# Attention fused with two dense layers: VectorE's splits, sums and weight conversion ordered behind evictions of scores, and dense work that starts one turn later

## The chip, the cores and the metric

One core of one Trainium2 chip. The metric is device microseconds of one execution. The kernel before has a median of 1105.09 us over 3 runs (1104.98 to 1105.69).

## What is computed

Inputs are q, k, v of 4 x 8 heads, 576 positions, 64 wide, and the weights of two dense layers. Everything is float32.

```python
scores = (1/8) * q @ k^T
scores = where(scores >= max(scores) - tau, scores, -1e9)
attn   = exp(scores - max(scores)); attn /= sum(attn) + 1e-9
x = (attn @ v), heads put side by side          # 2304 x 512
h = x @ w_in1;  x = where(h >= 1, h, where(h <= -1, 0, (h+1)^2/4)) @ w_out1
h = x @ w_in2;  x = (h * clip(h+3, 0, 6) / 6) @ w_out2
```

The dense layers go from 512 to 2048 and back to 512 features.

## The kernel before, in words

A dense product is made of three matmuls on operands that are each split in a high part (fp32r) and a low part. ScalarE makes the high part, VectorE or GpSimd subtracts it from the source for the low part.

**Attention** goes over 16 jobs (a batch and a pair of heads) of 5 steps each (four blocks of 128 queries, then the last 64 of both heads). One step: TensorE makes scores in two PSUM pairs P0 and P1 (`em_scores`, L380); VectorE evicts them to `p`, negated, with the row's maximum (L395: this is called an eviction below); ScalarE takes the exponential (`em_exp`, L408) and VectorE the threshold `th` (L411); VectorE masks and sums (`em_mask`, L417); TensorE transposes `p` (`em_pt`, `em_tail`, L294), ScalarE copies the result to `Gf` and `Gt` (L445, L448, L459, L463); every few steps ten pairs of matmuls multiply it by v (`pv_chunk`, L481). After a job VectorE adds 1e-9 to its sums `z` and inverts them (`pre_norm`, L500, L501). The scores of a step can't be written before the eviction of the step before has read the same PSUM pair.

**Dense work beside attention** (`dense1`, the first layer for the first three batches, in groups of 256 tokens): `split_x` splits x in `xh` (ScalarE, L704) and `xl` (VectorE, L705), four pairs in a round; `em_h` makes 12 matmuls of 256 columns into the one bank Q2 (L724), then ScalarE (L733, L734), VectorE (L735, tile `r`), ScalarE (`gh`, L741) and GpSimd (`gl`, L742) apply the gate; `em_part` multiplies by w_out (L786) into bank Q3, which is copied to `ob` when a round ends (L799 or L795). The next 12 matmuls of L724 can't begin before L735 has read Q2. Weights are converted on the way (`split_a`, `split_b`): ScalarE L124, L127, L145; GpSimd L128, L143, L147; VectorE L135 (shift) and L141 (sign).

**After attention** the rest of the dense work follows, with matmuls of 512 columns (L766, L1164 and others).

What sets the order: a scheduler in the framework places instructions by a model of time. `after(ins, prev)` adds an order without a semaphore ("ins not before prev" on the same engine). `pins` holds the last instruction of a kind: `S` the last exponential, `M` the last mask, `V` and `G` those of the dense gate. While attention runs, `split_x` put L704 behind `S` and L705 behind `M`; L135, L141 and L500 had no such pin on VectorE.

The main loop (`for _ in attention()`) gets a turn at every `yield` of attention. As soon as the four jobs of the first batch are done, `mode["mlp"]` is set and each turn gives `dense1` a credit of 0.57.

```python
for _ in attention():
    if not mode["mlp"]:
...
        if not ready(0):
            continue
        mode["mlp"] = True
    credit = min(credit + share, 3.0)
```

Of the kernel before, what the change touches and what calls it, by code (L numbers as in the profile page):

```python
# [11 lines left out]
ALU = mybir.AluOpType  # L12
# [6 lines left out]
def kernel(  # L19
# [89 lines left out]
            tc.add_manual_dep(ins.ins, prev.ins.name, mybir.DependencyInfo(kind, why), reason="pace")  # L109

    pe_pins = []
    pins = {"M": None, "S": None, "V": None, "G": None}

    def place_of(f, hl, dt, name):
        return (wbase if f < NF1 else wpool[f]).tile([128, 512], dt, tag=f"wi{hl}{f}", name=name)
# [1 line left out]
    def split_a(kind, m, f):  # L117
        t = wraw.pop((kind, m, f))
        pool = wbase if f < NF1 else wpool[f]
        hi = pool.tile([128, 512], F32R, tag=f"w{kind}h{f}", name=f"w{kind}h{f}")  # L120
        lo = pool.tile([128, 512], F32R, tag=f"w{kind}l{f}", name=f"w{kind}l{f}")
        c = stage.tile([128, 512], U32, tag="w_c", name="w_c", bufs=2)
        r = t[:, :, 0].bitcast(I32)
        x = S.activation(out=r, in_=t[:, :, 0], func=ACTF.Copy, scale=2.0 ** -29)  # L124
        after(x, pins["S"])
        if mode["att"]:
            after(S.activation(out=f32(c), in_=f32(t[:, :, 1]), func=ACTF.Abs), x)  # L127
            G.tensor_scalar(  # L128
                out=f32(c), in0=f32(c), scalar1=122879.9921875, scalar2=2.0 ** -15, op0=ALU.min, op1=ALU.max)
        else:  # L130
            S.activation(out=f32(c), in_=f32(t[:, :, 1]), func=ACTF.Abs)
            x = V.tensor_scalar(
                out=f32(c), in0=f32(c), scalar1=2.0 ** -15, scalar2=122879.9921875, op0=ALU.max, op1=ALU.min)
            after(x, pins["V"])
        V.tensor_scalar(out=c, in0=c, scalar1=3, scalar2=0x3FFFFFFF,  # L135
                        op0=ALU.logical_shift_left, op1=ALU.bitwise_and)
        wc[kind, m, f] = (hi, lo, c, t, r)

    def split_b(kind, m, f):
        hi, lo, c, t, r = wc.pop((kind, m, f))  # L140
        V.scalar_tensor_tensor(out=c, in0=t[:, :, 1], scalar=0xC0000000, in1=c,  # L141
                               op0=ALU.bitwise_and, op1=ALU.bitwise_or)
        x = G.tensor_tensor(out=c.bitcast(I32), in0=c.bitcast(I32), in1=r, op=ALU.add)  # L143
        after(x, pins["G"])
        x = S.activation(out=hi, in_=f32(c), func=ACTF.Copy)  # L145
        after(x, pins["S"])
        x = G.tensor_tensor(out=lo, in0=f32(c), in1=f32(hi), op=ALU.subtract)  # L147
        after(x, pins["G"])
        wsp[kind, m, f] = (hi, lo)
# [206 lines left out]
    def em_scores(j, i):  # L356

        last = i == NBLK - 1

        if not last:  # L360
            mode["s"] += 1
        ss = [unit_bank() for _ in range(1 if last else 2)]
        prev = None
        c = slice(i * 128, i * 128 + (TAIL if last else 128))
        thirds = j >= JR
        whole = thirds and last
        es = ((0, 0), (1, 1), (0, 1), (1, 0)) if last else ((0, 0), (1, 0), (0, 1), (1, 1))
        terms = ((qt, kt), (qt, kl), (ql, kt)) if thirds else ((qt, kt),)
        x = 0
        for pair in (((0, 0),), ((0, 1),)) if whole else (es[0:2], es[2:4]):  # L370
            for n, (a, w) in enumerate(terms):
                for h, e in pair:
                    r = slice(0, 128) if whole else slice(h * D, (h + 1) * D)
                    k0 = e * HS + (TAIL if last or h == 0 else 0)
                    if whole:
                        o, cs = ss[0][:, e, 0:HS], slice(MAIN, MAIN + 128)
                    else:
                        o, cs = ss[0][h * TAIL:(h + 1) * TAIL, e, 0:HS] if last else ss[h][:, e, 0:HS], c
                    with tc.high_priority(offset=900 if x else 0):
                        mm = T.matmul(o, a[j][r, cs], w[j][r, k0:k0 + HS], start=(n == 0), stop=(n == len(terms) - 1),  # L380
                                      skip_group_check=True)
                    after(mm, prev)
                    prev = mm
                    if x == 0:
                        pe_pins.append(mm)
                        for y in range(1 if last else 2):
                            after(mm, readers.get((mode["s"] - y) % 2), True)
                    x += 1
        nm = ap.tile([128, 2], F32, tag="nm", name="nm", bufs=3)
        th = ap.tile([128, 2], F32, tag="th", name="th", bufs=3)  # L390
        p = ap.tile([128, 2, 2, HS], F32, tag="p", name="p", bufs=3)
        if i == 0:
            zt[j] = ap.tile([128, 9], F32, tag="z", name="z", bufs=2)
        for x, s in enumerate(ss):
            reads(V.tensor_scalar(out=p[:, x], in0=s[:, :, 0:HS],  # L395
                                           scalar1=taus[:, 3:4] if j >= JR else -1.0, scalar2=3e38,
                                           op0=ALU.mult, op1=ALU.min, accum_out=nm[:, x:x + 1]), len(ss) - 1 - x)
        blk[j, i] = (p, nm, th, [])

    blk = {}  # L400
# [94 lines left out]
    def pre_norm(j):  # L495
        if j not in zt:
            return
        z = zt.pop(j)
        rz = rp[:, 0:9].unsqueeze(2) if j in OVER else ap.tile([128, 9, 1], F32, tag="rz", name="rz", bufs=2)
        V.tensor_scalar(out=z, in0=z, scalar1=1e-9, scalar2=None, op0=ALU.add)  # L500
        V.reciprocal(out=rz[:, :, 0], in_=z)  # L501
        rb = ap.tile([128, SEQ], F32, tag="rb", name="rb")
        if j in OVER:
            V.transpose(out=rq, in_=rp)
            rd = dram.tile([9, 128], F32, name=f"rd{j}")
            for a in range(4):
                nc.sync.dma_start(out=rd[:, 32 * a:32 * a + 32], in_=rq[32 * a:32 * a + 9, :])
            rbs[j] = (rd, rb)
            return
        rb = rb[:, 0:MAIN].rearrange("p (c h n) -> p c h n", c=4, h=2)  # L510
        for h in HEADS:
            G.tensor_scalar(out=rb[:, :, h, :], in0=rz[:, 4 * h:4 * h + 4, :].to_broadcast([128, 4, 64]),
                            scalar1=1.0, scalar2=0.0, op0=ALU.mult, op1=ALU.add)
        rbs[j] = (rz, rb)
# [164 lines left out]
    def split_x(key, kks=range(KD)):  # L679
        m, g, ph = key[:3]  # L680
        r = xs.setdefault(key, [])
        for kk in kks:
            if kk < len(r):
                continue
            b = g // 2 if ph == 1 else g
            if ph == 1:
                pool, n, bufs = mt, GRP, 1
                if all(b * HP + x in here for x in (kk, kk | 1)):
                    src = here[b * HP + kk][:, (g % 2) * GRP:(g % 2 + 1) * GRP]
                else:  # L690
                    if kk % 2 == 0:
                        t = mt.tile([128, 2, GRP], F32, tag="io", name="xst", bufs=2)
                        nc.sync.dma_start(out=t, in_=narrow(xd, g)[:, kk:kk + 2, :])
                    src = t[:, kk % 2]
            elif ph == 2 and g == NB - 1:
                pool, n, bufs = wide["x"], MAIN, 2
                src = here[b * HP + kk][:, 0:MAIN]
            else:
                pool, n, bufs = wide["x"], WIDE[g], 2
                src = wide["p"].tile([128, n], F32, tag="xst", name="xst", bufs=3)  # L700
                nc.sync.dma_start(out=src, in_=(x2d if m == 1 else xd)[g][:, kk, :])
            hi = pool.tile([128, n], F32R, tag=f"xh{kk}", name="xh", bufs=bufs)
            lo = pool.tile([128, n], F32R, tag=f"xl{kk}", name="xl", bufs=bufs)
            x = S.activation(out=hi, in_=src, func=ACTF.Copy)  # L704
            y = V.tensor_tensor(out=lo, in0=src, in1=f32(hi), op=ALU.subtract)  # L705
            if mode["att"]:
                after(x, pins["S"])
                after(y, pins["M"])
            r.append((hi, lo))

    def pin_mlp(mm):
# [277 lines left out]
    for _ in attention():  # L989
        if not mode["mlp"]:  # L990
            if mode["t"] == 3:
                weights.prefetch()
            if mode["t"] >= 5 and mode["step"]:
                mode["step"] = False
                if weights.done < FIRST and mode["t"] % 5 in (0, 4):
                    weights.half()
            if not ready(0):
                continue
            mode["mlp"] = True
        credit = min(credit + share, 3.0)  # L1000
        while credit > 0:
            c = next(part1)
# [388 lines left out]
```

## Time and profile before

| | |
|---|---|
| median of 3 runs | 1105.09 us |
| the profiled execution | 1104.55 us, its span 1102.8 us |
| TensorE matmuls busy | 1069.6 us (97%) |
| VectorE, ScalarE, GpSimd busy | 670.0, 641.3, 452.1 us |
| mean granted TensorE clock | 0.993 of full |

The span is what lies between the first and the last instruction; some 1.75 us of the execution lie around it. A view by windows gives busy time in a stretch; the view of waits tells for what an engine's idle time ended; the timeline shows single instructions, with the idle time before one in brackets and what ended it. `PEclk` is the mean granted TensorE clock in a stretch (1.00 is the level of 2.4 GHz, 0.50 would be 1.2 GHz throughout).

### The profile page before, as it was taken

Reading aid. Unit: us, or ns where it says so; the run is one execution under the profiler, and the core shown is the slowest. Engines: PE = TensorE matmul, PEld = TensorE weight load, DVE = VectorE, ACT = ScalarE, POOL = GpSimd, SP = SyncE. Lnnn points to the kernel's source line nnn. Section 1 sums busy time; section 2 is a strip of 40 time slices with the busy share of each in tenths; the row PEclk is TensorE's granted clock in tenths of the full one; section 3 lists DMA queues with packets and bytes.
Section 4 is the critical chain, followed back from the end, with each engine's and each line's share of the span. In section 5 each row is a group of like instructions: output and inputs, shape, how many; then the busy total and the mean of one; then the engine's idle time right before and its main releaser. Section 6 shows DMA issues by size and latency. Waiting matters only on the chain.

```text
span 1102.8 us, 18304 instructions
## 1 busy us (share of the span) xinstructions
PE 1069.6 (97%) x6514; PEld 876.3 (79%) x6514; DVE 670.0 (61%) x1313; ACT 641.3 (58%) x1271; POOL 452.1 (41%) x390
## 2 busy tenths in 40 slices
PE   7998889999999999999999999999999999999998
PEld 5555567778888888888889888888888888887887
DVE  5889998975776756355536855657788633333010
ACT  5777886776767767555557766555444433334221
POOL 0233767733222222155627665567623211112432
PEclk9999899999999999999999999999999999999999
DMA  6444545333322121125223555555455155449211
GB/s 170 121 96 104 130 103 149 70 73 82 72 61 66 45 62 42 32 67 161 88 88 124 174 182 190 170 174 170 125 182 190 53 187 161 157 149 374 66 39 58
DMA packets 175019, 132.54 MB, mean 120 GB/s; under 512 B 102736, under 2 KB 142416, under 8 KB 174928
## 3 DMA queue, kind: packets, MB, share of 16 engines
q1 hardware_dynamic: 173584, 131.08, 40.5%
q8 instruction: 51, 0.84, 0.3%
q10 hardware_dynamic: 1344, 0.30, 0.1%
q14 instruction: 40, 0.33, 0.1%
HBM read 93.00 MB, written 38.34 MB: 119 GB/s over the span
## 4 chain that ended last, share of the span: by engine, by line
PE 76%; issue 9%; DVE 8%; POOL 3%; ACT 3%; DMA 1%; SPq 0%; DVEq 0%; POOLq 0%; ACTq 0%
PE Q L724 25%; PE P L766 18%; PE Q L786 7%; PE Q L481 6%; PE P L380 5%; PE Q L294 5%; PE P L1164 4%; DVE p L395 2%; DVE p L417 2%; PE Q L1290 2%; PE Q L1301 2%; POOL gl L1153 2%; PE Q L1184 1%; DVE xl L705 1%; ACT e L408 1%
## 5 line engine op out<-in xcount | busy, mean ns | idle before, releaser
L742 POOL TENSOR_TENSOR gl<-r,gh 128x256 fp32r<-128x256 f32 (+1 forms) x142 | 154.4, 1088 | 290.9 <-ACT gh L741 279.4
L724 PE MATMUL Q<-xh,wih 128*128 128x256 f32 (+1 forms) x568 | 193.5, 341 | 2.5 <-DVE r L735 2.3
L724 PE MATMUL Q<-xl,wih 128*128 128x256 f32 (+1 forms) x568 | 188.9, 332 | 0.0
L724 PE MATMUL Q<-xh,wil 128*128 128x256 f32 (+1 forms) x568 | 188.8, 332 | 0.0
L417 DVE SCALAR_TENSOR_TENSOR p<-p,th,e 128x576 f32<-128x576 f32 x144 | 123.2, 877 | 15.5 <-ACT e L408 9.7
L408 ACT ACTIVATE e<-p,nm 128x576 f32<-128x576 f32 x144 | 109.4, 775 | 35.3 <-DVE p L395 34.4
L735 DVE SCALAR_TENSOR_TENSOR r<-r,Q 128x256 f32<-128x256 f32 (+1 forms) x110 | 54.8, 498 | 121.6 <-ACT r L734 117.6
L724 PEld LDWEIGHTS Q<-xh,wih 128*128 128x128 f32 x568 | 107.6, 189 | 20.3 <-DVE r L735 4.1
L741 ACT ACTIVATE gh<-r 128x256 fp32r<-128x256 f32 (+1 forms) x142 | 73.0, 515 | 82.4 <-DVE r L735 31.1
L294 PE MATMUL Q<-ident,p 128*128 128x128 f32 x656 | 106.9, 280 | 10.4 <-ACT Gf L445 8.1
L724 PEld LDWEIGHTS Q<-xl,wih 128*128 128x128 f32 x568 | 107.7, 190 | 10.3
L724 PEld LDWEIGHTS Q<-xh,wil 128*128 128x128 f32 x568 | 107.5, 189 | 10.2
L143 POOL TENSOR_TENSOR w_c<-w_c,w_raw 128x512 int32<-128x512 int32 x64 | 89.6, 1400 | 42.6 <-DVE w_c L141 21.8
L294 PEld LDWEIGHTS Q<-ident,p 128*128 128x128 f32 x656 | 73.7, 140 | 40.0 <-ACT Gf L445 14.3
L1153 POOL TENSOR_TENSOR gl<-r,gh 128x512 fp32r<-128x512 f32 x32 | 41.6, 1302 | 137.9 <-ACT gh L1152 137.9
L380 PE MATMUL P<-kt,qt 64*128 64x288 f32 (+2 forms) x508 | 83.8, 416 | 11.7 <-DVE p L395 9.6
L445 ACT ACTIVATE Gf<-Q 128x512 f32<-128x512 f32 x128 | 74.1, 594 | 15.9 <-PE Q L294 15.1
L1184 PE MATMUL Q<-xw,sw 128*128 128x512 f32 x336 | 80.7, 389 | 0.2 <-DVE C L1200 0.2
L733 ACT ACTIVATE r<-Q,half 128x256 f32<-128x256 f32 (+1 forms) x110 | 58.7, 535 | 32.4 <-PE Q L724 25.0
L786 PE MATMUL Q<-gh,woh 128*128 128x256 f32 x240 | 75.3, 314 | 1.4 <-DVE ob L799 1.4
L395 DVE TENSOR_SCALAR_CACHE_REDUCE p<-P 128x576 f32<-128x576 f32 x90 | 65.2, 750 | 17.2 <-PE Q L294 10.1
L1184 PEld LDWEIGHTS Q<-xw,sw 128*128 128x128 f32 x336 | 63.0, 188 | 13.5 <-DVE C L1200 0.4
(147 smaller groups left out, 2455.2 us busy)
## 6 DMA issues: line engine op xcount, KB each, us to landing
sw<-sd SPq DMA_DIRECT2D x88, 256.0 KB
w_raw<-in_moe_w_in_dram SPq DMA_DIRECT2D x32, 512.0 KB
w_raw<-in_moe_w_out_dram SPq DMA_DIRECT2D x32, 512.0 KB
sd<-wz SPq DMA_DIRECT2D x32, 256.0 KB
vn<-in_v_dram SPq DMA_DIRECT2D x32, 128.0 KB
x2p<-ob SPq DMA_DIRECT2D x16, 256.0 KB
x2d<-ob SPq DMA_DIRECT2D x16, 256.0 KB
sd<-wih SPq DMA_DIRECT2D x16, 256.0 KB
```

Of the source, the lines that this page charges most:

```text
L143: x = G.tensor_tensor(out=c.bitcast(I32), in0=c.bitcast(I32), in1=r, op=ALU.add)
L294: x = T.transpose(out, in_, ident)
L380: mm = T.matmul(o, a[j][r, cs], w[j][r, k0:k0 + HS], start=(n == 0), stop=(n == len(terms) - 1), skip_group_check=True)
L395: reads(V.tensor_scalar(out=p[:, x], in0=s[:, :, 0:HS], scalar1=taus[:, 3:4] if j >= JR else -1.0, scalar2=3e38, op0=ALU.mult, op1=ALU.min ...
L408: pins["S"] = S.activation(out=e, in_=p[:, x], func=ACTF.Exp, bias=nm[:, x:x + 1], scale=-1.0)
L417: pins["M"] = V.scalar_tensor_tensor(out=p[:, x], in0=p[:, x], scalar=th[:, x:x + 1], in1=e, op0=ALU.is_le, op1=ALU.mult, accum_out=zt[j][ ...
L445: S.activation(out=f[:, h, :, d0:d0 + 128], in_=tm.rearrange("p (c n) -> p c n", c=4), func=ACTF.Copy)
L724: mm = T.matmul(h, l[:, kk * 128:(kk + 1) * 128], r, start=(x == 0), stop=(x == 3 * KD - 1))
L742: y = G.tensor_tensor(out=gl, in0=r, in1=f32(gh), op=ALU.subtract)
L766: T.matmul(a, l, r, start=(first and x == 0), stop=(last and x == 2))
L786: mm = T.matmul(o, l, r, start=(f == fs[0] and x == 0 and i == 0), stop=(f == fs[-1] and x == 2 and i == 1), skip_group_check=True)
L1184: T.matmul(banks[role], t[:, l, c, :], r, start=(first and y == 0), stop=(y == 5), skip_group_check=True)
```

## The change

A new pin `E` holds the last eviction L395. While dense work runs beside attention, these steps of VectorE are put behind it: both VectorE steps of the weight conversion (L135, L141), the addition to `z` (L500) and the subtraction in `split_x` (L705). In the first round (`key[3]` is 0) `split_x` loses its old pins to `S` and `M`. And the turn in which the first batch becomes ready gives no credit: dense work begins with the next turn.

```diff
-    pins = {"M": None, "S": None, "V": None, "G": None}
+    pins = {"E": None, "M": None, "S": None, "V": None, "G": None}
...
-        V.tensor_scalar(out=c, in0=c, scalar1=3, scalar2=0x3FFFFFFF,
-                        op0=ALU.logical_shift_left, op1=ALU.bitwise_and)
+        x = V.tensor_scalar(out=c, in0=c, scalar1=3, scalar2=0x3FFFFFFF,
+                            op0=ALU.logical_shift_left, op1=ALU.bitwise_and)
+        if mode["mlp"] and mode["att"]:
+            after(x, pins["E"])
...
+        x = V.scalar_tensor_tensor(out=c, in0=t[:, :, 1], scalar=0xC0000000, in1=c,
+                                   op0=ALU.bitwise_and, op1=ALU.bitwise_or)
+        if mode["mlp"] and mode["att"]:
+            after(x, pins["E"])
...
+            pins["E"] = V.tensor_scalar(out=p[:, x], in0=s[:, :, 0:HS],
...
+            reads(pins["E"], len(ss) - 1 - x)
...
-        V.tensor_scalar(out=z, in0=z, scalar1=1e-9, scalar2=None, op0=ALU.add)
+        after(V.tensor_scalar(out=z, in0=z, scalar1=1e-9, scalar2=None, op0=ALU.add), pins["E"] if mode["mlp"] else None)
...
             if mode["att"]:
-                after(x, pins["S"])
-                after(y, pins["M"])
+                if key[3]:
+                    after(x, pins["S"])
+                    after(y, pins["M"])
+                after(y, pins["E"])
...
             mode["mlp"] = True
+            continue
```

No instruction of an engine that computes is added or taken away. Lines below L135 move down in the changed file: L141 becomes L143, L294 L298, L380 L384, L395 L399, L411 L416, L417 L422, L481 L486, L500 L505, L705 L710, L724 L731, L735 L742, L799 L806.

VectorE where dense work begins, step 25 of attention (the step whose scores lie in P_1404 and P_1405, in the changed program in P_1375 and P_1376), before:

```order
L135 TENSOR_SCALAR w_c<-w_c 128x512
L417 SCALAR_TENSOR_TENSOR p,z<-p,th,e 128x576
L705 TENSOR_TENSOR xl<-xu,xh 128x256 x3
L141 SCALAR_TENSOR_TENSOR w_c<-w_raw,w_c 128x512
L705 TENSOR_TENSOR xl<-xu,xh 128x256
L500 TENSOR_SCALAR z<-z 128x9
L395 TENSOR_SCALAR p,nm<-P_1404 128x576
L395 TENSOR_SCALAR p,nm<-P_1405 128x576
```

and in the changed program:

```order
L135 TENSOR_SCALAR w_c<-w_c 128x512
L422 SCALAR_TENSOR_TENSOR p,z<-p,th,e 128x576
L399 TENSOR_SCALAR p,nm<-P_1375 128x576
L399 TENSOR_SCALAR p,nm<-P_1376 128x576
L505 TENSOR_SCALAR z<-z 128x9
L710 TENSOR_TENSOR xl<-xu,xh 128x256 x4
L143 SCALAR_TENSOR_TENSOR w_c<-w_raw,w_c 128x512
L416 TENSOR_SCALAR th<-nm,taus 128x2
L506 RECIPROCAL rp<-z 128x9
L422 SCALAR_TENSOR_TENSOR p,z<-p,th,e 128x576 x2
```

The two evictions now precede six steps that stood ahead of them; those six stand ahead of the same step's masks instead.

TensorE after the first 12 matmuls of dense work, in the changed program:

```order
L731 MATMUL Q_1425<-xl,wih_361 128x256
L731 MATMUL Q_1425<-xh,wil_362 128x256
L298 MATMUL Q_1504<-ident,p 128x128
L486 MATMUL Q_1507<-Gf,vn_120 64x320 x8
L486 MATMUL Q_1507<-Gt,vn_120 64x320 x2
L384 MATMUL P_1593<-kt,qt 128x288
L384 MATMUL P_1594<-kt,qt 128x288
```

These scores (step 27, in P_1593 and P_1594) follow the product with v at once. Before, four transposes and the second 12 matmuls of L724 stood between the two; they now come behind the scores. By the order of all of TensorE, 24 matmuls of L724 precede the scores of step 27 before and 12 in the changed program. The distance of 12 is still there at the scores of step 36: 132 of L724 and 60 of L786 before, 120 and 60 now.

VectorE where the first round's product leaves bank Q3 (L799, L806 in the changed file), before:

```order
L735 SCALAR_TENSOR_TENSOR r<-r,Q_2000 128x256
L705 TENSOR_TENSOR xl<-xu,xh 128x256
L135 TENSOR_SCALAR w_c<-w_c 128x512
L705 TENSOR_TENSOR xl<-xu,xh 128x256 x2
L141 SCALAR_TENSOR_TENSOR w_c<-w_raw,w_c 128x512
L705 TENSOR_TENSOR xl<-xu,xh 128x256
L799 COPY ob<-Q_1763 128x512
```

and in the changed program:

```order
L135 TENSOR_SCALAR w_c<-w_c 128x512
L742 SCALAR_TENSOR_TENSOR r<-r,Q_1903 128x256
L143 SCALAR_TENSOR_TENSOR w_c<-w_raw,w_c 128x512
L742 SCALAR_TENSOR_TENSOR r<-r,Q_2007 128x256
L710 TENSOR_TENSOR xl<-xu,xh 128x256 x2
L806 COPY ob<-Q_1770 128x512
L710 TENSOR_TENSOR xl<-xu,xh 128x256
```

Between the `r` that precedes it and the copy stand two steps now, where six stood.

## Rows read from the trace of the kernel before

**Rows 1.** The page: busy time by engine, granted clock in 40 slices.
```profile
PE 1069.6 (97%) x6514; PEld 876.3 (79%) x6514; DVE 670.0 (61%) x1313; ACT 641.3 (58%) x1271; POOL 452.1 (41%) x390
...
PEclk9999899999999999999999999999999999999999
```

**Rows 2.** Windows, six stages: us; busy of each engine; clock; DMA share, GB/s.
```profile
0.00:105.00 105.00, 92.66 (x653) 58.81 (x653) 85.97 (x233) 75.95 (x152) 27.02 (x36) 1.00 0.51 122
105.00:155.00 50.00, 40.55 (x265) 28.06 (x267) 48.66 (x109) 41.02 (x90) 32.69 (x27) 0.90 0.49 121
155.00:180.00 25.00, 21.44 (x154) 17.11 (x151) 20.27 (x40) 19.16 (x46) 20.57 (x19) 0.93 0.62 143
180.00:230.00 50.00, 48.99 (x380) 39.57 (x380) 43.20 (x94) 36.29 (x81) 32.85 (x28) 1.00 0.36 94
230.00:475.00 245.00, 243.42 (x2027) 207.32 (x2024) 154.73 (x406) 167.00 (x370) 63.18 (x62) 1.00 0.22 56
475.00:1102.80 627.80, 622.57 (x3047) 525.44 (x3045) 317.13 (x433) 301.88 (x536) 275.75 (x221) 1.00 0.46 146
```

**Rows 3.** Waits of TensorE, 105 to 475 us: total, times, longest.
```profile
PE Q L294 <- ACT Gf L445: 5.2, 5, 2.0
PE P L380 <- DVE p L395: 3.7, 2, 2.1
PE Q L724 <- DVE r L735: 2.3, 2, 1.6
PE Q L786 <- DVE ob L799: 1.4, 1, 1.4
...
PE Q L294 <- DVE p L417: 0.8, 1, 0.8
```

**Rows 4.** Timeline of TensorE: start, us, what, idle before and its end.
```profile
90.29 2.37 PE L481 MATMUL Q<-Gf,vn 128*64 128x320 f32 x16
...
106.01 1.24 PE L380 MATMUL P<-kt,qt 64*128 64x288 f32 x8 [1.16 <-DVE xu L555]
...
111.71 2.29 PE L380 MATMUL P<-kt,qt 64*128 64x288 f32 x8 [2.15 <-DVE p L395]
...
115.14 3.93 PE L481 MATMUL Q<-Gf,vn 128*64 128x320 f32 x16
...
145.68 2.29 PE L380 MATMUL P<-kt,qt 64*128 64x288 f32 x8 [1.56 <-DVE p L395]
...
176.88 0.58 PE L786 MATMUL Q<-gh,woh 128*128 128x256 f32 x1 [1.38 <-DVE ob L799]
```

**Rows 5.** Timeline of VectorE where dense work begins.
```profile
106.98 1.09 DVE L705 TENSOR_TENSOR xl<-xu,xh 128x256 fp32r<-128x256 f32 x3
107.99 0.68 DVE L141 SCALAR_TENSOR_TENSOR w_c<-w_raw,w_c 128x512 uint32<-128x512 uint32 x1
...
108.93 1.26 DVE L500 TENSOR_SCALAR z<-z 128x9 f32<-128x9 f32 x1
110.22 0.76 DVE L395 TENSOR_SCALAR_CACHE_REDUCE p<-P 128x576 f32<-128x576 f32 x1
...
113.07 1.53 DVE L417 SCALAR_TENSOR_TENSOR p<-p,th,e 128x576 f32<-128x576 f32 x1 [0.22 <-ACT e L408]
```

**Rows 6.** Timeline of VectorE at the two later stalls.
```profile
140.54 1.84 DVE L705 TENSOR_TENSOR xl<-xu,xh 128x256 fp32r<-128x256 f32 x2
...
144.20 0.74 DVE L395 TENSOR_SCALAR_CACHE_REDUCE p<-P 128x576 f32<-128x576 f32 x1
...
176.15 0.68 DVE L799 COPY ob<-Q 128x512 f32<-128x512 f32 x1
```

**Rows 7.** Groups by line on VectorE, 105 to 230 us: busy, mean ns; idle before.
```profile
L395 DVE TENSOR_SCALAR_CACHE_REDUCE p<-P 128x576 f32<-128x576 f32 x33 | 23.7, 746 | 2.8 <-PE Q L294 2.5 <-PE P L380 0.2
L141 DVE SCALAR_TENSOR_TENSOR w_c<-w_raw,w_c 128x512 uint32<-128x512 uint32 x16 | 14.1, 882 | 0.1
L135 DVE TENSOR_SCALAR w_c<-w_c 128x512 uint32<-128x512 uint32 x16 | 12.1, 758 | 0.5 <-POOL w_c L128 0.5
```

More of the change, by code (lines that the diff above doesn't have):

```diff
@@ L140, in split_b @@
         hi, lo, c, t, r = wc.pop((kind, m, f))
-        V.scalar_tensor_tensor(out=c, in0=t[:, :, 1], scalar=0xC0000000, in1=c,
-                               op0=ALU.bitwise_and, op1=ALU.bitwise_or)
+        x = V.scalar_tensor_tensor(out=c, in0=t[:, :, 1], scalar=0xC0000000, in1=c,
+                                   op0=ALU.bitwise_and, op1=ALU.bitwise_or)
+        if mode["mlp"] and mode["att"]:
+            after(x, pins["E"])
         x = G.tensor_tensor(out=c.bitcast(I32), in0=c.bitcast(I32), in1=r, op=ALU.add)
@@ L394, in em_scores @@
         for x, s in enumerate(ss):
-            reads(V.tensor_scalar(out=p[:, x], in0=s[:, :, 0:HS],
+            pins["E"] = V.tensor_scalar(out=p[:, x], in0=s[:, :, 0:HS],
                                            scalar1=taus[:, 3:4] if j >= JR else -1.0, scalar2=3e38,
-                                           op0=ALU.mult, op1=ALU.min, accum_out=nm[:, x:x + 1]), len(ss) - 1 - x)
+                                           op0=ALU.mult, op1=ALU.min, accum_out=nm[:, x:x + 1])
+            reads(pins["E"], len(ss) - 1 - x)
         blk[j, i] = (p, nm, th, [])
```

## The prediction

> **What bounds the kernel now.** I read the page first: TensorE's matmuls are busy 97% of the span, and the clock row has a 9 in every slice but the fifth; the loss is small and sits early [rows 1]. The table by windows then says where. From 230 us on TensorE is busy 243.42 of 245 us and 622.57 of 627.8 us: nothing that VectorE does there can bring much. From 0 to 105 us it is idle 12.3 us, but dense work hasn't begun and the new pins don't act. What is left is the stretch in which dense work begins: idle are 50 - 40.55 = 9.45 us from 105 to 155 us, 25 - 21.44 = 3.56 us to 180 us, 1.0 us to 230 us and 1.6 us to 475 us [rows 2]. The mean granted clock is 0.90 and 0.93 in the first two of these, so the 1.2 GHz level also took up to 0.10 x 50 + 0.07 x 25 = 6.75 us [rows 2]. All that the change can reach is therefore 9.45 + 3.56 + 1.0 + 1.6 = 15.6 us of idle time and some 6.75 us of clock.
>
> The second thing to see is VectorE in the same windows: 48.66 of 50 us busy, then 20.27 of 25 us [rows 2]. Where TensorE is idle most, VectorE is full. An order among VectorE's steps moves no work away; it decides what TensorE waits for last. The waits name that: 5.2 us for ScalarE's copies `Gf`, 3.7 us for evictions (L395), 2.3 us for the gate's `r` (L735), 1.4 us for the copy `ob` [rows 3]. Only the evictions, `r` and `ob`, together 7.4 us, are VectorE's own; the change favours the first at the expense of the second.
>
> **The change, term by term** (signs: plus is time saved).
>
> *Start, step 25.* Before, the scores end at 106.01 + 1.24 = 107.25 us [rows 4], and the first eviction starts at 110.22 us, behind four L705, L141 and L500 that fill the 3.24 us from 106.98 us [rows 5]. TensorE waits 2.15 us for it and runs the next scores at the low level, 2.29 us against 1.24 us [rows 4]. With the change the evictions start at 107.25 us. The gain is not 2.97 us, for the six steps now precede the masks, and TensorE soon waits for a mask's transpose, behind which the product with v stands in its order. I walk VectorE: 107.25, two evictions at 0.75 (1.5) give 108.75; `z` between 0.15 (an estimate from 1.26, which was taken while GpSimd worked) and 1.26; four L705 at 1.09 / 3 (1.45); L141 0.68; `th` and the reciprocal 0.3 (an estimate); two masks between 1.64 (twice the ordinary 0.82) and 2.35 (0.82 + 1.53) [rows 5]. The masks end between 112.97 and 114.79 us. The product with v, which started at 115.14 us, starts at about 113.1 to 114.9 us: 0.2 to 2.0 us gained. At the 2.4 GHz level it takes 2.37 us, as at 90.29 us, in place of 3.93 us [rows 4], if the clock doesn't fall: another 0 to 1.56 us. I take **+2.0** between 0.2 and 3.6, because TensorE's waits before it fall from one long to two shorter ones.
>
> *The dense group that falls back.* The second 12 matmuls of L724 now wait behind the scores of step 27 and for `r` of the group before, since there is one bank Q2. `r` follows step 26's evictions, masks and one weight conversion: 1.5 + 0.82 to 1.53 for a mask, twice, + 0.76 + 0.88 [rows 5, 7] is 4.8 to 6.2 us, and what TensorE does meanwhile (product 2.37 to 3.93, scores 1.24 [rows 4], some transposes) is 3.6 to 5.8 us. The wait lies between 0 and 2.6 us: **-1.0**. The group itself isn't lost: its 12 matmuls run later, where TensorE is busy, and before they ran where it had nothing else.
>
> *Steps 30 and 31.* The eviction at 144.20 us came behind four splits, two of which took 1.84 us [rows 6]; TensorE waited 1.56 us and ran the scores 1.05 us slower [rows 4]. In the changed order four splits (1.84 and two at 0.36) leave that place, and one more mask (0.82) and L500 with its two followers enter (0.15 to 1.26, and 0.4 for the two, an estimate): the eviction comes 0.1 to 1.2 us earlier, and where the wait goes, the clock's 1.05 us may go too. Saved is between 0.1 and 2.3 us: **+1.0**.
>
> *The copy `ob`.* It started at 176.15 us, and TensorE had waited 1.38 us for it [rows 6, 4]; the clock cost up to 1.75 us in this window [rows 2]. Six steps stood between it and the `r` before, now two. L135 (0.76), L141 (0.88) [rows 7] and two L705 (0.36 each) go from in front of it, 2.4 us, more than the wait; but the two remaining splits wait for ScalarE. **+1.5**, between 0 and 3.1.
>
> *The rest.* The longest wait for `r`, 1.6 us, lies near 304 us, behind splits too; there the changed order puts a transpose ahead of `r` and takes `z` away: 0, between -0.75 and +1.5. ScalarE makes three splits of round 0 long before 105 us, where it is busy 75.95 of 105 us [rows 2]: 0, down to -1.0 if each delays an exponential by 0.35 us. `z` is inverted some 2 us later; its user comes four steps on, hence 0. The later start of one turn costs 0, as the amount of dense work is the same. From about 460 us on TensorE's order is the old one.
>
> **Sum:** 2.0 - 1.0 + 1.0 + 1.5 = 3.5 us. The profiled execution took 1104.55 us, so 1101.05 us; it is 0.54 us under the median of 1105.09 us, so I predict 1105.09 - 3.5 = **1101.6 us**. The lower ends of all terms together are 0.2 - 2.6 + 0.1 + 0 - 0.75 - 1.0 = -4.1 us, the upper ones 3.6 + 0 + 2.3 + 3.1 + 1.5 = 10.5 us; they won't all fall on one side.
>
> A rule weighed against this: an eviction took 0.746 us in the mean of 33, as much as one by itself (0.74 at 144.20 us), while the shift L135 and L141 took 0.758 and 0.882 us in the mean, L141 0.68 us at 107.99 us, where GpSimd had nothing to do [rows 5 to 7]. The Trainium skill (SBUF — State Buffer, "Who interferes with whom") says that VectorE and GpSimd share a port pair as an exclusive lock: a VectorE step with two SBUF inputs or in a two-port mode waits for a whole GpSimd instruction or holds one up, a `tensor_scalar` that also writes its accumulator doesn't take the pair. The rows agree. By that rule the steps that grow are those that now stand together ahead of `r`, while at the start, where GpSimd is idle, nothing is won by it: the second term comes out at its lower end, the others stay, and the sum is 2.0 - 2.6 + 1.0 + 1.5 = 1.9 us, 1103.2 us.
>
> **Rivals.**
>
> 1. *Forecast, 48%.* The stalls from 105 to 180 us close in part: 1098 to 1103.5 us.
> 2. *VectorE's total decides, 22%.* It is 97% busy to 155 us [rows 2], so masks, and all that follows from them, come no earlier; evictions come early and wait for nothing. The waits change name, L395 to L417, and the 0.8 us for masks [rows 3] grow by what the evictions lose. Only clock and `ob` remain, or nothing: 1103 to 1106 us. Two of four splits in round 1 still precede the following evictions, so the order does less than its pins say. Against it: at 155 to 180 us VectorE is idle 4.7 of 25 us, so there is slack to turn into time.
> 3. *`r` becomes the wait, 18%.* One Q2 bank lets no group begin until `r` has left VectorE's queue. Evictions and masks of a step, 1.5 + 1.64 us, now come ahead of it. If in the ten steps from 105 to 180 us each group waits 0.9 us longer, that is 9 us against the gains of 2.0 + 1.0 + 1.5: 4.5 us slower, 1109.6 us. It decides from 0.45 us a group on. For it: 2.3 us of such waits in 105 to 475 us [rows 3] with an order that was not against `r`. Against it: after 180 us VectorE has 6.8 of 50 us free, and a late group only lets other work ahead.
> 4. *Nearly all closes, 12%.* With TensorE never idle long enough for the clock to fall, 8 of 13.0 us of idle time up to 180 us and 4 of 6.75 us of clock return: 12 us, 1093 us. Against it: the largest wait, 5.2 us for `Gf`, is ScalarE's.
>
> **How the numbers follow.** About 0.2%, 2.2 us, is what a measurement of this kernel can tell from no change: below 1102.9 us is faster, above 1107.3 us slower. Of the first case 43 of 48 parts are faster and 5 the same; of the second 2 are faster, 18 the same, 2 slower; of the third 2 the same and 16 slower; the fourth is all faster: 43 + 2 + 12 = 57% faster, 25% the same, 18% slower. The range leaves out the far half of the third and of the fourth case, about 9% and 8%: 1095.0 to 1108.0 us. The forecast's own range is that of its case.
>
> **What would show it.** Right: in the window from 105 to 155 us TensorE is idle under 8 us and the clock above 0.92; no wait of 2 us for an L399 at the start; the wait for `ob` gone; from 230 us on every stage starts some 3 us earlier with its own length unchanged. Wrong on the second case: the idle time to 155 us stays at 9 us, named after masks or `Gf`. Wrong on the third: waits of L731 for L742 rise from 2.3 us to over 6 us.

## The result and the profile after

The changed kernel takes 1121.99 us (median of 4 runs, 1119.86 to 1124.4) against 1105.03 us of the kernel before (4 runs, 1104.25 to 1105.69): a ratio of 1.0149 [1.0136, 1.0162], 17.0 us slower. The forecast was 3.5 us faster, with a range that ended at 1108.0 us. The profiled execution took 1124.40 us, its span is 1122.6 us.

The table of windows of the changed kernel, with the columns of [rows 2], says where:

```profile
0.00:105.00 105.00, 83.93 (x552) 53.30 (x554) 72.53 (x199) 66.42 (x133) 22.48 (x33) 0.94 0.48 114
105.00:155.00 50.00, 43.62 (x293) 28.21 (x290) 44.91 (x110) 38.12 (x79) 26.44 (x22) 0.91 0.49 109
155.00:180.00 25.00, 20.95 (x129) 14.52 (x131) 23.16 (x50) 19.42 (x44) 18.39 (x17) 0.86 0.42 123
180.00:230.00 50.00, 46.73 (x361) 38.20 (x358) 39.64 (x86) 37.54 (x84) 31.70 (x30) 1.00 0.45 109
230.00:475.00 245.00, 241.55 (x2002) 203.00 (x2002) 167.52 (x429) 171.19 (x374) 70.29 (x68) 1.00 0.24 59
```

The first line is the surprise: from 0 to 105 us TensorE is idle 21.07 us instead of 12.34 us, its clock is 0.94 instead of 1.00, and VectorE has done 199 instructions instead of 233 [rows 2]. The prediction had passed over this stretch. TensorE's waits from 0 to 110 us name the place (us in total, times, longest):

```profile
PE Q L486 <- ACT Gf L450: 8.9, 3, 4.1
PE P L384 <- DVE p L399: 6.7, 10, 1.5
```

The first of them doesn't exist before. What held ScalarE's copies `Gf` is in ScalarE's timeline, at two of three places (start, us, what, idle before and what ended it):

```profile
40.42 0.42 ACT L709 ACTIVATE xh<-xu 128x256 fp32r<-128x256 f32 x1 [3.48 <-POOL xu L541]
40.75 0.76 ACT L413 ACTIVATE e<-p,nm 128x576 f32<-128x576 f32 x1
...
64.78 0.42 ACT L709 ACTIVATE xh<-xu 128x256 fp32r<-128x256 f32 x1 [4.24 <-POOL xu L541]
...
91.89 0.42 ACT L709 ACTIVATE xh<-xu 128x256 fp32r<-128x256 f32 x1 [1.83 <-POOL xu L541]
```

These are the splits of round 0 that lost their pin to the last exponential. Each stands in ScalarE's queue ahead of an exponential (at the third place a copy `Gf` stands between) and waits for GpSimd's normalisation. At the first two places GpSimd itself waits for the reciprocals that come back over DMA (`rb`); at the third the profile names another DMA, a load of q:

```profile
39.00 1.40 POOL L541 TENSOR_TENSOR xu<-xu,rb 128x576 f32<-128x576 f32 x1 [9.46 <-DMA rb<-rd]
63.36 1.40 POOL L541 TENSOR_TENSOR xu<-xu,rb 128x576 f32<-128x576 f32 x1 [10.23 <-DMA rb<-rd]
```

The exponential at 40.75 us reads an eviction that had ended by 37.3 us, and still began only behind the split: a split of 0.42 us held the exponential, the copies behind it and all that needs them. In TensorE's timeline the product with v waits, and two of the three then run longer than the 1.95 us that the first of them took before (at 38.14 us):

```profile
42.53 3.27 PE L486 MATMUL Q<-Gf,vn 128*64 128x256 f32 x16 [3.33 <-ACT Gf L450]
...
66.89 3.68 PE L486 MATMUL Q<-Gf,vn 128*64 128x256 f32 x16 [4.09 <-ACT Gf L450]
...
92.84 1.95 PE L486 MATMUL Q<-Gf,vn 128*64 128x256 f32 x16 [1.49 <-ACT Gf L450]
```

The windows around the first two, and around the third, show TensorE's clock in the last column but two:

```profile
42.00:47.00 5.00, 4.47 (x24) 2.33 (x24) 4.55 (x13) 4.49 (x9) 1.36 (x2) 0.67 0.04 9
66.00:71.00 5.00, 4.11 (x19) 2.22 (x19) 4.57 (x12) 4.55 (x9) 1.32 (x1) 0.50 0.10 31
92.00:95.00 3.00, 2.16 (x20) 1.35 (x20) 1.50 (x5) 3.00 (x7) 0.72 (x1) 1.00 0.37 60
```

0.50 is the level of 1.2 GHz throughout; before, the clock is 1.00 in this whole stretch [rows 2]. So the two longer waits are paid twice, once as idle time and once as matmuls at the lower clock behind it. From 0 to 105 us TensorE is idle 8.7 us longer than before, and a clock of 0.94 for 105 us is up to 6.3 us more: together 15.0 us.

To see when the loss arises I set the start of each eviction against that of the same eviction before (us later; profiled executions; the first eviction is 0.0 to 1.1 us off already, by kernel). A profiled execution can lie off its kernel's median: that of the changed kernel took 2.4 us more, that of e9 2.1 us less, that of e11 3.5 us more.

| eviction of step | 0 | 8 | 13 | 23 | 25 | 30 | 35 | 40 | 78 |
|---|---|---|---|---|---|---|---|---|---|
| changed kernel | 1.0 | 4.0 | 8.0 | 15.1 | 12.2 | 13.3 | 16.9 | 16.1 | 17.5 |
| e1 splits of ScalarE pinned | 0.8 | 0.9 | -0.5 | -0.1 | -3.1 | 0.2 | 6.8 | 7.9 | 6.2 |
| e2 ScalarE's splits free, alone | 0.1 | 3.8 | 8.1 | 13.5 | 12.4 | 12.4 | 14.0 | 13.6 | 13.6 |
| e3 pins behind evictions, alone | 0.1 | 0.2 | -1.1 | -0.5 | -1.7 | -1.4 | -0.8 | 2.1 | 0.7 |
| e4 later turn, alone | 0.7 | 0.7 | -0.4 | 0.1 | -2.3 | 0.8 | 8.1 | 6.2 | 2.1 |
| e5 one split free | 0.8 | 4.1 | 5.6 | 6.0 | 6.0 | 6.7 | 6.9 | 6.5 | 6.5 |
| e6 splits early but not too early | 0.0 | 0.0 | -0.1 | 1.2 | -1.7 | 0.0 | 9.2 | 11.8 | 11.2 |
| e9 VectorE's splits free, alone | 0.3 | 0.3 | -1.0 | -0.6 | -0.6 | 2.2 | 8.0 | 9.4 | 9.1 |
| e14 credit 1.0 more | 1.1 | 1.1 | -0.3 | 0.2 | -0.8 | 1.2 | 8.0 | 8.1 | 13.9 |
| e15 credit 0.33 more | 0.5 | 0.5 | -0.1 | 0.3 | 0.3 | 0.7 | 0.8 | 3.4 | 5.2 |

The changed kernel loses 14.1 us from the first eviction to step 23, wins 2.9 us at the start of dense work (15.1 to 12.2), loses 5.3 us by step 78, and 2.3 us behind it (its span is 19.8 us longer). The table tells when attention comes, not what TensorE does meanwhile; *The second loss* returns to that.

### The profile page after: what moved, and what is told of

Read it like the earlier page. It is cut to its first block, busy times and chain, and to the rows that moved or that the text cites. A ratio compares the mean times of both kernels' runs of the same rounds, so it can differ in the third digit from the quotient of the medians.

```text
span 1122.6 us, 18308 instructions
## 1 busy us (share of the span) xinstructions
PE 1079.2 (96%) x6514; PEld 880.1 (78%) x6514; DVE 670.3 (60%) x1313; ACT 644.9 (57%) x1271; POOL 448.0 (40%) x390
## 4 chain that ended last, share of the span: by engine, by line
PE 74%; DVE 3%; DMA 2%; issue 1%; ACT 1%; POOL 0%; SPq 0%; DVEq 0%; POOLq 0%
PE Q L731 23%; PE P L773 18%; PE P L1172 7%; PE Q L1192 7%; PE Q L793 6%; PE Q L486 4%; PE Q L298 3%; PE P L384 3%; PE Q L1298 2%; PE Q L1309 2%; DVE p L422 1%; DVE p L399 1%; DMA r<-rr 0%; DMA sw<-sd 0%; DVE raw L308 0%
## 5 line engine op out<-in xcount | busy, mean ns | idle before, releaser
L731 PE MATMUL Q<-xh,wih 128*128 128x256 f32 (+1 forms) x568 | 193.5, 341 | 3.5 <-DVE r L742 2.5
L731 PE MATMUL Q<-xl,wih 128*128 128x256 f32 (+1 forms) x568 | 189.2, 333 | 0.0
L731 PE MATMUL Q<-xh,wil 128*128 128x256 f32 (+1 forms) x568 | 188.9, 333 | 0.0
L422 DVE SCALAR_TENSOR_TENSOR p<-p,th,e 128x576 f32<-128x576 f32 x144 | 131.3, 932 | 23.4 <-ACT e L413 18.3
L742 DVE SCALAR_TENSOR_TENSOR r<-r,Q 128x256 f32<-128x256 f32 (+1 forms) x110 | 54.7, 497 | 139.9 <-ACT r L741 133.8
L731 PEld LDWEIGHTS Q<-xh,wih 128*128 128x128 f32 x568 | 107.8, 190 | 23.1 <-DVE r L742 4.7
L298 PE MATMUL Q<-ident,p 128*128 128x128 f32 x656 | 107.0, 284 | 11.5 <-ACT Gf L450 6.1
L731 PEld LDWEIGHTS Q<-xl,wih 128*128 128x128 f32 x568 | 107.9, 190 | 10.6 <-DVE xl L710 0.4
L731 PEld LDWEIGHTS Q<-xh,wil 128*128 128x128 f32 x568 | 107.8, 190 | 10.2
L298 PEld LDWEIGHTS Q<-ident,p 128*128 128x128 f32 x656 | 74.9, 142 | 39.9 <-issue 14.2
L384 PE MATMUL P<-kt,qt 64*128 64x288 f32 (+2 forms) x508 | 84.2, 418 | 11.5 <-DVE p L399 10.7
L486 PE MATMUL Q<-Gf,vn 128*64 128x320 f32 (+1 forms) x512 | 75.9, 437 | 9.3 <-ACT Gf L450 8.9
L399 DVE TENSOR_SCALAR_CACHE_REDUCE p<-P 128x576 f32<-128x576 f32 x90 | 65.4, 751 | 23.1 <-PE P L384 14.7
```

Of the source, the lines that this page charges most:

```text
L298: x = T.transpose(out, in_, ident)
L422: pins["M"] = V.scalar_tensor_tensor(out=p[:, x], in0=p[:, x], scalar=th[:, x:x + 1], in1=e, op0=ALU.is_le, op1=ALU.mult, accum_out=zt[j][ ...
L486: mm = T.matmul(o[h * D:(h + 1) * D], vn[j % 2][:, c, h, :], f[:, h, c] if c < 4 else t, start=(c == 0), stop=(c == 4), skip_group_check=True)
L731: mm = T.matmul(h, l[:, kk * 128:(kk + 1) * 128], r, start=(x == 0), stop=(x == 3 * KD - 1))
```

## The experiments

Each was timed beside the kernel before. "Before" is 1104.34 us for e1 to e4, 1105.35 us for e5 to e8, 1104.87 us for e9 to e11 and 1104.75 us for e13 to e15.

### The parts of the change

**e1.** The changed kernel, with the pin of ScalarE's splits put back for round 0.

```diff
+                after(x, pins["S"])
                 if key[3]:
-                    after(x, pins["S"])
                     after(y, pins["M"])
```

> The changed kernel with one line back: ScalarE's split xh is ordered behind the last exponential in round 0 too; everything on VectorE and the later turn stay as changed. Theory A (ScalarE's three splits of round 0 stand too early in its queue and hold it for 3.5, 4.2 and 1.8 us until GpSimd has normalised x; evictions are 14.1 us late before dense work begins): 14 us of the loss of 17 go, about 1106 to 1109 us. Theory B (VectorE's new order delays the gate's r and the masks): the loss stays, 1118 to 1124 us. Theory C (the later turn leaves TensorE empty): the same as B.

Measured: 1113.2 us, ratio 1.0079 [1.0066, 1.0093]. The loss before step 23 is gone (-0.1 us in the table), but only half of the 17 us with it, so the time lies between the ranges of theory A and theory B: another loss shows between steps 25 and 40.

**e2.** The kernel before, with this pin alone taken away for round 0.

```diff
-                after(x, pins["S"])
+                if key[3]:
+                    after(x, pins["S"])
```

> The kernel before with the pin of xh behind the exponential taken away in round 0 alone; no E pin, no later turn, xl still behind the masks. Theory A: 11 to 16 us slower than before, 1116 to 1121 us. Theories B and C: 1105 us within 1 us.

Measured: 1118.6 us, ratio 1.0129 [1.0115, 1.0143], so 14.3 us for three instructions of 0.42 us. It is there at step 23 (13.5 us); nothing is added later.

**e3.** The kernel before with the pins behind evictions (`pins["E"]`) alone.

> The kernel before with the E pins alone (L135, L141, L500, L705 behind the last eviction); old pins of the splits kept, no later turn. Theory A: between 3 us faster and 3 us slower than before, as its share is what is left of 17 us after 14. Theory B: 10 to 17 us slower. Theory C: no change.

Measured: 1105.68 us, ratio 1.001 [1.0002, 1.0019]. TensorE's waits from 105 to 475 us in e3:

```profile
PE Q L298 <- DVE p L422: 3.5, 2, 1.8
PE Q L298 <- ACT Gf L450: 3.3, 3, 1.7
PE P L384 <- DVE p L399: 2.2, 3, 1.0
PE Q L730 <- DVE r L741: 1.6, 2, 1.4
PE Q L792 <- DVE ob L805: 1.6, 2, 1.4
```

Waits for evictions fell from 3.7 to 2.2 us, those for masks rose from 0.8 to 3.5 us [rows 3]: the wait changed its name. By the traces TensorE's order differs from that of before only from 148.6 to 319.3 us, and as many dense matmuls stand ahead of each transpose of attention until 200 us as before.

**e4.** The kernel before with the later turn alone.

```diff
             mode["mlp"] = True
+            continue
```

> The kernel before with the later turn alone: no credit in the turn in which the first batch becomes ready. Theory A: between 3 us faster and 3 us slower. Theory B: no change. Theory C: 10 to 17 us slower.

Measured: 1109.88 us, ratio 1.005 [1.0036, 1.0064], 5.5 us slower, which none of the three theories had in its range. The start wins 2.4 us (0.1 to -2.3), and more is lost behind it. Its first large stall in TensorE's timeline:

```profile
122.43 0.33 PE L294 MATMUL Q<-ident,p 128*128 128x128 f32 x1 [3.71 <-ACT Gf L445]
```

and ScalarE's timeline just before it:

```profile
119.36 0.63 ACT L145 ACTIVATE wih<-w_c 128x512 fp32r<-128x512 f32 x1 [1.87 <-POOL w_c L143]
...
121.26 0.63 ACT L145 ACTIVATE woh<-w_c 128x512 fp32r<-128x512 f32 x1 [0.91 <-POOL w_c L143]
121.80 0.58 ACT L445 ACTIVATE Gf<-Q 128x512 f32<-128x512 f32 x1
```

This looks like the pattern of round 0's splits: two splits of weights wait for GpSimd ahead of the copy that TensorE needs. No run took them away alone.

### Is it the wait in the queue?

**e5.** The kernel before, with one of the three splits free.

```diff
-                after(x, pins["S"])
+                if key[3] or kk:
+                    after(x, pins["S"])
```

> The kernel before, with one of round 0's three early splits on ScalarE (kk = 0) left without its pin, the other two pinned as before. Theory A (each freed split stands in ScalarE's queue ahead of an exponential and holds everything behind it while GpSimd waits for the round trip; 3.5, 4.2 and 1.8 us of wait make the 14.3 us of three freed splits): about a third of 14.3 us, so 1108.5 to 1110.5, with one wait of ScalarE for L536 of 3 to 4 us near 40 us and none near 65 and 92. Rival (the loss comes from the new order of the other engines that a moved split brings, whatever its number): 1112 or above, or within 1 us of before.

Measured: 1110.46 us, ratio 1.0039 [1.0026, 1.0052]; the medians are 5.1 us apart. In the traces this moves one instruction, on ScalarE, from the 152nd to the 43rd of its 1,271 places; the orders of the other engines are those of before. Its row:

```profile
40.51 0.42 ACT L704 ACTIVATE xh<-xu 128x256 fp32r<-128x256 f32 x1 [3.73 <-POOL xu L536]
```

A wait of 3.73 us makes a delay of 5.2 us at step 23 (6.0 less the first eviction's 0.8), which is still there at step 78; and it costs a third of e2.

**e6.** The changed kernel, with round 0's splits pinned behind the exponentials of steps 9, 14 and 19 (`exps` holds each step's exponential).

```diff
                 if key[3]:
                     after(x, pins["S"])
                     after(y, pins["M"])
+                elif kk < 3:
+                    after(x, exps[NBLK * kk + 9])
```

> The changed kernel, with round 0's three early splits on ScalarE pinned behind the exponential of steps 9, 14 and 19: still far earlier than before, yet some two steps after GpSimd's normalisation is done. Theory A (the wait in the queue is what costs, not the early place or the 0.42 us of work): no wait of ScalarE for L541 over 0.5 us and a delay at step 23 of under 3 us; the time that of the changed kernel with pinned splits, 1110 to 1114. Rival (work added to ScalarE before 105 us costs by itself, or the split of VectorE does): 1117 to 1122, the delay at step 23 10 us or more without such a wait.

Measured: 1117.51 us, ratio 1.0109 [1.0093, 1.0125]. The splits in ScalarE's timeline:

```profile
44.60 0.43 ACT L711 ACTIVATE xh<-xu 128x256 fp32r<-128x256 f32 x1
...
65.36 0.43 ACT L711 ACTIVATE xh<-xu 128x256 fp32r<-128x256 f32 x1
...
87.05 0.42 ACT L711 ACTIVATE xh<-xu 128x256 fp32r<-128x256 f32 x1
```

They are about as early as in the changed kernel and wait for nothing; the delay at step 23 is 1.2 us instead of 15.1. That settles the first cause: the wait costs, not the early place nor the work. The time missed theory A's range all the same and lies in the rival's, whose delay of 10 us at step 23 didn't come: the loss lies behind it, 11.8 us at step 40.

### The second loss

**e7.** e4, with the share of the turn that is left out given to the next one.

```diff
             mode["mlp"] = True
+            credit = share
+            continue
```

> The kernel before with the later turn alone, and the dense share of the turn left out credited to the next one, so that from there on TensorE's queue holds as many dense matmuls as before. Theory C1 (a group of 12 dense matmuls less in every step to fill TensorE's waits until 230 us makes the 5.5 us of the later turn): 1104 to 1106, PE busy of 105 to 230 us back at 110 to 111 us. Theory C2 (the new order of ScalarE's queue, in which splits of weights stand ahead of evictions and wait for GpSimd, makes it; how much is dense matters little): 1108 to 1111, again with waits of over 2 us for Gf.

Measured: 1117.27 us, ratio 1.0106 [1.0092, 1.012]. It was to repay filler and cost some 6 us more than e4; both ranges missed. Its order shows that the credit did not do what it was meant to: up to 175 us nearly all transposes of attention have as many dense matmuls ahead of them as in e4 or fewer, and only behind that more. TensorE is busy 103.49 us from 105 to 230 us, against 110.98 us before, so theory C1 was not put to the test; waits of over 2 us for `Gf` (the longest 3.7 us) came as in C2.

**e8.** e1 without the later turn; what is left beside e3 is that VectorE's splits of round 0 lose their old pin to the last mask.

> The changed kernel without the later turn and with ScalarE's splits of round 0 pinned as before: the pins behind evictions alone, VectorE's splits of round 0 free of their old pin. If the costs stand apart (freed splits and later turn), what is left is that of the pins behind evictions, 1105.7, so 1104.5 to 1107; if VectorE's freed splits of round 0 cost something of their own, they show here as 1108 or more. Rival by the prediction's terms (start, copy of the result and steps 30 and 31 gain 3 to 4 us when the other two parts are gone): 1101 to 1103.

Measured: 1112.52 us, ratio 1.0062 [1.0049, 1.0074]; so these splits cost something of their own.

**e9.** The kernel before with that alone.

```diff
-                after(y, pins["M"])
+                if key[3]:
+                    after(y, pins["M"])
```

> The kernel before, with only VectorE's part of round 0's splits (xl) left without its old pin; ScalarE's splits, the start and all other pins as before. It moves 384 of TensorE's 5,996 matrix operations, all between the start of dense work and 237 us. Theory D (what e8 paid beyond the pins behind evictions, 6.8 us, is these freed splits of VectorE: a new order of all four engines until 237 us with other waits in it): 1110 to 1114, TensorE idle some 6 us longer between 105 and 230 us, and nothing lost before 105 us or after 237. Rival (they cost only together with the pins behind evictions, which put them behind other work): 1104 to 1107.

Measured: 1115.34 us, ratio 1.0095 [1.0082, 1.0108]: 10.5 us, a little above theory D's range, with nothing lost before step 25. TensorE is idle 4.6 us longer from 105 to 230 us.

**e10, e11.** The kernel before with `share = 0.58`, and with `share = 0.56`.

> The kernel before with the dense share per turn at 0.58 in place of 0.57 and nothing else: a change that has nothing to do with the one studied, and moves TensorE's order from its 866th matrix operation (some 190 us) to the end of attention. Theory E (the order before was the best of many, and any other order of the same instructions from 105 us on costs some microseconds): 1107 to 1113. Rival (the losses of e1, e4, e6, e7 and e8 come from something that the later turn and the freed splits have in common, not from being another order): 1103 to 1106.5.

> The same with the share at 0.56, which moves TensorE's order from its 863rd matrix operation on. Theory E: 1107 to 1113. Rival: 1103.5 to 1107, as there is a little less dense work beside attention and as much more behind it.

Measured: 1110.65 us, ratio 1.0058 [1.0046, 1.007], and 1105.9 us, ratio 1.0013 [1.0004, 1.0023]. Neither differs by more than 1 us from before up to step 35; TensorE's orders begin to differ at 189 us. Theory E's range holds e10, the rival's holds e11.

**e13, e14, e15.** The kernel before, with 0.57, 1.0 and 0.33 more credit at the first turn of dense work.

```diff
             mode["mlp"] = True
+            credit = 0.57
```

> The kernel before, where the first turn of dense work has 0.57 more credit; start, pins and all else as before. In TensorE's order the dense work stands one group of 12 matrix operations later against attention from the second step of dense work on (12, 24, 24, 42 operations in place of 24, 36, 36, 54), as in e4 and e9, without the later turn and without a freed split. Theory F (what the later turn and VectorE's freed splits cost is this lag, which leaves TensorE without filler while VectorE decides until about 200 us): 1109 to 1116, as e4, e8 and e9. Rival (each had its own accident): no reason for a loss, 1103 to 1107.

> The same with 1.0 more credit. Here TensorE's order does not lag (24, 36, 42, 54 dense matrix operations against 24, 36, 36, 54 before), yet it is another order over the same stretch, with 30 more dense operations ahead of the attention step at 200 us, as in e8 and e9. Theory F: 1102 to 1107. Theory E (any other order of this stretch costs): 1108 to 1114.

> The same with 0.33 more credit. TensorE's order is that of before until about 200 us and differs in small moves behind it. Theory F: 1103 to 1107. Theory E: 1106 to 1111, as e10.

Measured: 1114.67 us, ratio 1.0091 [1.0076, 1.0106]; 1117.36 us, ratio 1.0111 [1.0097, 1.0125]; 1107.97 us, ratio 1.003 [1.0019, 1.0041]. Theory F, the lag of one group, falls with e14, which has no lag at the start and loses the most of the three. Theory E does better, in a narrower form that was drawn from the results. The number of dense matmuls that TensorE's order has ahead of each transpose of attention tells the kernels apart. Where it differs from the kernel before until 189 us, by whatever edit (e1, e4, e6, e7, e8, e9, e13, e14), the evictions fell back by 5.8 to 9.7 us from step 30 to step 35, in the changed kernel by 3.6 us. Where it is the same (e2, e3, e5, e10, e11, e15), by no more than 1.6 us.

At step 35 a round of dense work ends; ScalarE's splits for the next (tile `xh`) overwrite what the round's last matmuls read, VectorE's splits wait for ScalarE's, and the next evictions stand behind VectorE's. Before, ScalarE's splits find TensorE done; ScalarE's timeline of the kernel before, and VectorE's up to the eviction of step 35:

```profile
172.29 1.02 ACT L704 ACTIVATE xh<-xu 128x256 fp32r<-128x256 f32 x3
```

```profile
172.72 1.02 DVE L705 TENSOR_TENSOR xl<-xu,xh 128x256 fp32r<-128x256 f32 x1 [1.75 <-ACT xh L704]
...
177.08 0.74 DVE L395 TENSOR_SCALAR_CACHE_REDUCE p<-P 128x576 f32<-128x576 f32 x1
```

In e9 they wait for TensorE's dense matmuls; ScalarE's and VectorE's timelines of e9:

```profile
181.51 1.14 ACT L704 ACTIVATE xh<-xu 128x256 fp32r<-128x256 f32 x3 [1.86 <-PE Q L725]
```

```profile
181.97 0.92 DVE L705 TENSOR_TENSOR xl<-xu,xh 128x256 fp32r<-128x256 f32 x1 [1.23 <-ACT xh L704]
...
185.09 0.75 DVE L395 TENSOR_SCALAR_CACHE_REDUCE p<-P 128x576 f32<-128x576 f32 x1
```

It is tempting to see the same cause again, a split that waits ahead of attention's work. The same splits begin at 171.5 to 173.1 us in e3, e10, e11, e15 and the kernel before, without a wait for TensorE, and at 177.4 to 184.1 us in e1, e4, e6, e7, e8, e9, e13 and e14, in six of these with one, of 0.27 to 2.21 us. But two of the eight have no such wait, in e9 it is 1.86 us where the splits are 9 us later, and VectorE's wait for ScalarE is shorter in e9 (1.23 us) than before (1.75 us).

The windows of the kernel before from the first eviction of step 30 to that of step 35, and on to that of step 40, with the columns of [rows 2], say what TensorE did:

```profile
138.60:177.10 38.50, 31.46 (x219) 23.06 (x218) 33.74 (x74) 30.24 (x71) 27.11 (x24) 0.95 0.49 118
177.10:213.50 36.40, 36.18 (x273) 29.93 (x273) 32.16 (x68) 26.30 (x57) 27.37 (x25) 0.96 0.40 106
```

and of e9:

```profile
140.80:185.10 44.30, 37.64 (x258) 27.74 (x258) 37.13 (x77) 34.63 (x78) 33.16 (x30) 0.92 0.50 130
185.10:222.80 37.70, 34.19 (x252) 26.88 (x251) 32.53 (x66) 26.45 (x58) 25.33 (x23) 0.95 0.33 86
```

Up to step 35 TensorE is idle 6.7 us in e9 and 7.0 us before: the evictions come later because TensorE does more first. In the eight kernels 34 to 59 more dense matmuls begin in this stretch than the 88 of before (undisturbed ones begin 0.12 us apart, so some 4 to 7 us, an estimate), and its idle time changes by -1.0 to +2.1 us. The idle time grows behind it: from step 35 to step 40 by 3.1 to 5.8 us in each of the eight, where 27 to 42 dense matmuls fewer begin than the 160 of before; by 0.3 to 1.3 us in the six, and by 0.6 us in the changed kernel. The longest wait there ends with one of ScalarE's copies (`Gf`, `Gt`, `xu`) in seven of the eight, in e6 with `r`. Some is lost earlier: from step 25 to step 30 TensorE's idle time grows by 0.7 to 4.3 us in the eight, by 0.0 to 1.8 us in the six. So the second loss is in the main idle time of TensorE in these two stretches; in some of the eight more time at the lower clock comes with it (e9: 0.84 from 105 to 155 us, against 0.90 before [rows 2]). That dense matmuls done before step 35 are then missing to fill the waits behind it fits these counts; no run tried it alone. Why these orders wait longer from step 25 on, and what makes the scheduler place a round's matmuls so, stays open.

No version beat the kernel before; the nearest are e3 (+1.3 us) and e11 (+1.0 us).

## Why the prediction was wrong

**The step that failed first** is in *The rest*: "ScalarE makes three splits of round 0 long before 105 us ...: 0, down to -1.0 if each delays an exponential by 0.35 us". It priced a moved step at its busy time. What it cost was its wait, 3.48, 4.24 and 1.83 us in the changed kernel, and the lower clock behind the longer two: 14.1 us by step 23, and 14.3 us in all when tried alone (e2). The diff and the order showed the step ahead of exponentials; what was missing was to ask when its input is ready, and GpSimd's row of that input was in the trace (38.78 us, after 10.24 us of idle time that a DMA ended). The first paragraph's "dense work hasn't begun and the new pins don't act" had ruled the stretch out before that question came up: the new pins don't act there, but the pins taken away did.

**The second** is "The later start of one turn costs 0, as the amount of dense work is the same." Alone it cost 5.5 us (e4). The amount is the same, the order isn't: in every run but the changed kernel itself in which other numbers of dense matmuls stand ahead of attention's transposes until 189 us, TensorE was idle 3.1 us longer or more from step 35 to step 40. Which wait makes this is not shown. That VectorE's splits lose their old pin got no price at all; alone it cost 10.5 us (e9). The parts don't add: 1.3 + 14.3 + 5.5 + 10.5 = 31.6 us against the 17.0 us measured. The last two change the order of the same stretch: with the pins behind evictions they cost 8.9 us together (e1), not 17.3. ScalarE's freed splits add only 8.1 us to e1; with them most of e1's loss behind step 35 is not there (TensorE is idle 0.8 us from step 35 to step 40, in e1 4.8 us), and why stays open.

**The terms of the sum.** *Start, step 25* (+2.0): right in kind. TensorE's wait for the first eviction fell from 2.15 to 0.83 us in the changed kernel and 0.97 us in e3, and the delay fell by 2.9 us from step 23 to step 25. The product with v starts 6.95 us behind the end of the step's scores in place of 7.89 us, so 0.9 us earlier, within the forecast 0.2 to 2.0 us, and takes 3.32 us in place of 3.93 us. (The walk left some 0.1 us between masks and product, where the rows of before have 0.5 us.) But a transpose then waits 2.44 us in TensorE's timeline of the changed kernel; the profile names `rq`, which VectorE makes at 128.85 us, here right behind the two masks:

```profile
123.89 1.24 PE L384 MATMUL P<-kt,qt 64*128 64x288 f32 x8 [0.83 <-DVE p L399]
...
129.08 0.30 PE L298 MATMUL Q<-ident,p 128*128 128x128 f32 x1 [2.44 <-DVE rq L509]
```

In e3 the start won 1.2 us (from -0.5 to -1.7). *The copy `ob`* (+1.5): in e3 its wait stayed at 1.4 us, so this term was 0; in the changed kernel the wait is gone, with everything around it moved. *Steps 30 and 31* (+1.0): e3's wait for the eviction of step 31 fell from 1.56 to 0.98 us, but its evictions gained nothing there (-1.7 at step 25, -1.4 at step 30, -1.1 at step 31). *The dense group that falls back* (-1.0) was no loss of its own that a run could show.

**The rivals.** For the pins behind evictions alone, rival 2 came nearest, both in time (1103 to 1106 us; e3: 1105.68 us, 1.3 us above its own before) and in its sign: waits pass from L395 to L417. Rival 3 named the wrong wait: those for `r` are 2.5 us in the changed kernel from 105 to 475 us against 2.3 us [rows 3]. No rival held what came, a split that waits for another engine ahead of attention's work. Of the checks, the idle time from 105 to 155 us (6.38 us), the wait at the start and that for `ob` were met, the clock of that window (0.91, not above 0.92) and the later stages weren't; they all named windows behind 105 us, where the larger part of the loss isn't. The rule that the prediction weighed, which set the sum at 1103.2 us, has no part in the first loss, whose waits end with a DMA. For the second no run tested it: VectorE's masks took 131.3 us in all in the changed kernel against 123.2 us before, for a cause that stays open.

## What to carry to other kernels

Price a step that moves forward in a queue by when its input is ready, not by its length: here what stood behind it on its engine waited as long as it did, and behind the two longer waits TensorE paid a second time at the lower clock. A scheduler that is left free can put a step ahead of a DMA round trip, as here; a pin taken away deserves the same look as one that is added. In a stretch where one engine is nearly full (VectorE, 48.66 of 50 us from 105 to 155 us [rows 2]), an edit that only reorders it has a price too, to be measured: here 1.0 to 12.6 us for a first credit or a share that adds no work. And a stream that comes later is not yet time lost: see whether the engine that bounds the kernel was idle or did other work first.

## What the runs showed that I hadn't expected

One instruction of 0.42 us, moved to another place in ScalarE's queue with nothing else changed, cost 5.1 us of 1105 us (e5). In the changed kernel TensorE's product began 2.1 us behind the split at both longer waits: the copy that it needs stands behind split and exponential in ScalarE's queue. Behind a wait of 3.33 and 4.09 us the product with v took 3.27 and 3.68 us, behind one of 1.49 us it took 1.95 us.
